# A planned attention and mixture kernel: other queue times for the factor spreads, another seed and number of planner passes, and 63-column constant matmuls in TensorE's planned gaps

## The chip, the cores and the metric

The kernel runs on one core of one Trainium2 chip. The metric is the device time of one execution in microseconds (us). All times of the trace come from one profiled execution.

## The reference, cut to what matters

Inputs are q, k and v of 4 batches, 12 heads, 448 positions and 64 columns, all float32. Attention comes first, then two feed-forward blocks on 1792 tokens of 768 columns; the output of the second is the result.

```python
q_n, k_n = rmsnorm(q, g_q), rmsnorm(k, g_k)          # x / sqrt(mean(x*x) + 1e-6) * g
scores = (q_n @ k_n.T) / sqrt(64)
scores = scores - max(scores)
attn = exp(scores);  attn = attn / (sum(attn) + 1e-9)
x = attn @ v                                          # 1792 x 768 after heads are joined
h = x @ moe_w_in                                      # 768 -> 2048
x = where(h > 0, h, exp(min(h, 0)) - 1) @ moe_w_out   # 2048 -> 768
xn = x / sqrt(mean(x*x) + 1e-6) * rms_g
g = xn @ w_gate;  silu = g / (1 + exp(-g))            # 768 -> 1536
out = (silu * (xn @ w_val)) @ moe2_w_out              # 1536 -> 768
```

## The kernel before, in words

**The work.** Every float32 operand is split into a high and a low part, and each product is made of three matmuls (high by high, high by low, low by high); much of the second half uses a scheme of seven products in place of eight. Attention is done in 24 pairs of heads, six pairs for each batch: `prep_q` and `prep_k` make the split operands `qh` and `ql` of a pair from the raw tile `rw`, `s_group` makes the scores in the banks 0 to 3 of PSUM (448 columns of 512), VectorE (DVE in the profile) takes the maximum of each row, ScalarE (ACT) the exponentials with their row sums (into `pj` and `p` for one parity of pairs, into `tbig` and `gbig` for the other), TensorE (PE) transposes these through the banks 4 to 6 into `pt` and `pe`, and multiplies with `rv`. The feed-forward work of a batch can start when its six pairs are done and `xf` is split into `xs`. The stages are: first block for batch 0, then for batch 1, second block for batches 0 and 1, first block for 2 and 3, second block for 2 and 3. Attention of batches 1 to 3 is laid between feed-forward matmuls; attention of batch 0 has nothing beside it. This is the lead-in, which ends at the first matmul on `xs`.

**The factors.** The key's norm factors `rr` must be there for every position in all 64 partitions of a head. `spread(i)` does that from pair 2 on by a write of `rr` to DRAM (`scr`) and two broadcast reads into `rb` (128 KB each), in SyncE's (SP) queue for the pairs 2 to 5 and in ACT's from then on. VectorE then multiplies `rw` with `rb` in place (`prep_k`, one SCALAR_TENSOR_TENSOR of 128x512). `sums(i)` does the same with the row sums (`rsum` to `rsb`).

**Weights.** `w_convert` (line 790) loads a compressed weight of 768 KB (`wr` from `wst`), makes `wc` from its upper part and the low half of `wt` from its bytes (each on ACT or on GpSimd, POOL), the high half of `wt` and the joining of both on VectorE. `w` and its low part are then copied from `wc`.

**The planner.** All of this is first entered into a class `Plan` (lines 34 to 300): each operation with the engines that could do it and a price for each, what it reads and writes. `schedule()` makes an order from a start rank with noise from `SEED`, then goes forward and backward `PASSES` times and keeps the order with the shortest modelled span. `forward()` is a list scheduler: an engine that is free takes the ready operation of lowest rank; an operation with two engines goes to the one that the model says is free sooner. `dma()` gives a transfer its modelled time. `issue()` writes all instructions out in the order of the planned starts; so the model's prices set the order and the engine of each instruction, and nothing of the model is left at run time. The string `LEAD` sets the first rank of batch 0's attention steps.

**Constant matmuls.** In planned gaps of TensorE `issue()` writes matmuls of ones by ones of 128 columns, whose result nothing reads. They go to bank 5, up to the planned start of the first instruction that uses bank 5 (`self.first_use`).

All instructions carry line 344 in the trace, since a wrapper at that line issues them; tiles name them.

## Time and profile before

| | us |
|---|---|
| median of 3 runs | 1232.96 |
| lowest and highest run | 1228.6, 1235.3 |
| profiled execution, its own time | 1231.14 |
| its span in the trace | 1229.3 |
| PE busy | 1205.9 (98%) |
| PE weight loads busy | 1013.6 (82%) |
| DVE, ACT, POOL busy | 907.4, 715.5, 836.6 |

The mean granted TensorE clock was 0.995 of full speed. The profile's busy share of PE counts pipelined matmuls, whose ends are modelled. The share is an average over stages that differ: the lead-in, where attention stands alone, has its own limits, and the feed-forward stages have theirs.

### The profile page before, as it was taken

Reading aid. Unit: us, or ns where it says so; the run is one execution under the profiler, and the core shown is the slowest. Engines: PE = TensorE matmul, PEld = TensorE weight load, DVE = VectorE, ACT = ScalarE, POOL = GpSimd, SP = SyncE. Lnnn points to the kernel's source line nnn. Section 1 sums busy time; section 2 is a strip of 40 time slices with the busy share of each in tenths; the row PEclk is TensorE's granted clock in tenths of the full one; section 3 lists DMA queues with packets and bytes.
Section 4 is the critical chain, followed back from the end, with each engine's and each line's share of the span. In section 5 each row is a group of like instructions: output and inputs, shape, how many; then the busy total and the mean of one; then the engine's idle time right before and its main releaser. Section 6 shows DMA issues by size and latency. Waiting matters only on the chain.

```text
span 1229.3 us, 18750 instructions
## 1 busy us (share of the span) xinstructions
PE 1205.9 (98%) x6270; PEld 1013.6 (82%) x6270; DVE 907.4 (74%) x1520; ACT 715.5 (58%) x1456; POOL 836.6 (68%) x713
## 2 busy tenths in 40 slices
PE   8999999999999999999999999999999989999998
PEld 6557867777777876777999998999999988899997
DVE  7877789898544469655598799948654799577667
ACT  6986878778765478665565565846534742322121
POOL 3467778788665686435998788866564877577484
PEclk9999999999999999999999999999999999999999
DMA  7678777776443468755599799767621266877767
GB/s 255 200 233 270 260 258 243 241 250 201 146 134 113 145 209 290 261 175 190 179 322 356 253 347 366 252 217 238 192 83 52 65 177 188 231 214 196 218 202 218
DMA packets 120164, 265.52 MB, mean 216 GB/s; under 512 B 15742, under 2 KB 59012, under 8 KB 120068
## 3 DMA queue, kind: packets, MB, share of 16 engines
q1 hardware_dynamic: 90260, 205.79, 49.5%
q0 software_dynamic: 21168, 49.55, 14.1%
q10 hardware_dynamic: 8640, 8.99, 2.6%
q8 instruction: 49, 0.80, 0.3%
q14 instruction: 47, 0.39, 0.1%
HBM read 183.11 MB, written 81.17 MB: 215 GB/s over the span
## 4 chain that ended last, share of the span: by engine, by line
PE 75%; DVE 8%; DMA 6%; ACT 4%; POOL 4%; issue 3%; ACTq 0%; SPq 0%; DVEq 0%; POOLq 0%
PE bank L344 75%; DMA wr<-wst 3%; POOL w L344 2%; DVE bank L344 2%; DVE tbig L344 1%; DVE wt L344 1%; DVE wc L344 1%; DVE gbig L344 1%; ACT tbig L344 1%; DVE ss L344 1%; ACT p L344 1%; DMA rsb<-rsum 1%; ACT wc L344 1%; DMA rw<-qk 1%; DMA rb<-scr 1%
## 5 line engine op out<-in xcount | busy, mean ns | idle before, releaser
L344 PE MATMUL bank<-xs,w 128*128 128x448 f32 x1731 | 396.8, 371 | 2.6 <-POOL xs L344 0.8
L344 PE MATMUL bank<-gbig,w 128*128 128x448 f32 x1603 | 362.4, 370 | 1.9 <-DVE gbig L344 0.8
L344 PEld LDWEIGHTS bank<-xs,w 128*128 128x128 f32 x1731 | 319.2, 188 | 35.6 <-issue 6.9
L344 PEld LDWEIGHTS bank<-gbig,w 128*128 128x128 f32 x1603 | 295.7, 188 | 31.8 <-issue 5.6
L344 POOL TENSOR_TENSOR w<-wc,w 128x768 fp32r<-128x768 f32 (+1 forms) x112 | 208.7, 1865 | 58.2 <-ACT w L344 47.7
L344 PE MATMUL bank<-late,w 128*128 128x448 f32 x647 | 162.8, 368 | 0.3 <-DMA w<-bout_S 0.3
L344 DVE TENSOR_REDUCE bank<-bank 128x1 f32<-128x448 f32 x168 | 98.9, 624 | 49.5 <-PE bank L344 49.1
L344 PEld LDWEIGHTS bank<-late,w 128*128 128x128 f32 x647 | 122.4, 189 | 10.5 <-ACT ybig L344 0.6
L344 ACT ACTIVATE p<-bank,nm,rr 128x448 f32<-128x448 f32 x126 | 90.0, 717 | 35.9 <-DVE nm L344 27.8
L344 DVE SCALAR_TENSOR_TENSOR wc<-wc,wt 128x768 int32<-128x768 int32 x68 | 88.8, 1306 | 13.9 <-ACT wc L344 9.7
L344 ACT ACTIVATE pt<-bank 128x384 f32<-128x384 f32 (+2 forms) x174 | 75.8, 451 | 33.3 <-PE bank L344 26.2
L344 POOL TENSOR_SCALAR w<-wc 128x768 fp32r<-128x768 f32 (+1 forms) x50 | 47.2, 945 | 58.8 <-PE bank L344 46.8
L344 DVE TENSOR_SCALAR wt<-wr 128x768 uint16<-128x768 uint16 x68 | 73.8, 1085 | 0.7 <-DMA wr<-wst 0.2
L344 ACT ACTIVATE wc<-wr 128x768 f32<-128x768 f32 x57 | 52.0, 912 | 37.7 <-DMA wr<-wst 17.8
L344 ACT ACTIVATE w<-wc 128x768 fp32r<-128x768 f32 (+1 forms) x75 | 59.0, 788 | 24.5 <-PE bank L344 23.0
L344 DVE TENSOR_TENSOR ybig<-bank,ybig 128x448 f32<-128x448 f32 x72 | 44.4, 618 | 38.6 <-PE bank L344 38.4
L344 PE MATMUL bank<-ident,p 128*128 128x128 f32 x441 | 71.5, 281 | 1.2 <-ACT rt L344 0.4
L344 ACT ACTIVATE tbig<-bank 128x448 f32<-128x448 f32 x85 | 45.9, 541 | 44.8 <-PE bank L344 31.3
L344 PEld LDWEIGHTS bank<-ident,p 128*128 128x128 f32 x441 | 54.2, 143 | 19.3 <-ACT pt L344 5.5
L344 DVE TENSOR_TENSOR tbig<-bank,tbig 128x448 f32<-128x448 f32 x93 | 56.0, 617 | 11.4 <-PE bank L344 10.6
L344 ACT ACTIVATE wt<-wr 128x768 uint16<-128x768 uint8 x49 | 53.4, 1090 | 15.5 <-DVE wc L344 13.0
L344 POOL TENSOR_TENSOR w<-p,w 128x768 fp32r<-128x768 f32 x28 | 54.2, 1939 | 12.0 <-ACT w L344 11.7
(271 smaller groups left out, 2233.7 us busy)
## 6 DMA issues: line engine op xcount, KB each, us to landing
wr<-wst SPq DMA_DIRECT2D x68, 768.0 KB
wc<-kept SPq DMA_DIRECT2D x64, 384.0 KB
kept<-wc SPq DMA_DIRECT2D x52, 384.0 KB
w<-bgv_S POOLq DMA_DIRECT2D x38, 384.0 KB, 3.9
bgv_A<-w SPq DMA_DIRECT2D x36, 384.0 KB
bgv_S<-w SPq DMA_DIRECT2D x32, 384.0 KB
rw<-qk SPq DMA_DIRECT2D x21, 512.0 KB
w<-bgv_A POOLq DMA_DIRECT2D x28, 384.0 KB, 4.0
```

What stands on the lines that cost most here:

```text
L344: return lambda *a, **k: f(*[real(x) for x in a], **{n: real(x) for n, x in k.items()})
```

## The change

The planner gets another seed and another number of passes, and its model is changed in two places. In `dma()` the broadcast reads of the factors get a modelled time that is 2.9 times (SP queue) or 1.4 times (ACT queue) as long, those of the row sums 2.0 or 1.2 times. In `forward()` an operation of DVE that uses the port shared with POOL, and that is planned while POOL issues a DMA, is priced to end only after that issue plus `AFTER`; before, a DMA issue of POOL counted as any other operation of POOL. Neither adds an instruction; both move where instructions stand and which engine does them.

In `issue()` constant matmuls are also written after bank 5 is in use, up to planned time 29.0. These late ones have 63 columns and go to the columns 449 to 511 of bank 3, behind the 448 columns that hold scores.

```diff
-    PASSES = 18
-    SEED = 7
+    PASSES = 13
+    SEED = 20
...
+    AFTER = 0.5
...
-    IDLE = (1.2, 0.3, 4.6)
+    IDLE = (1.2, 0.3, 4.6, 29.0, 0.125)
...
-            if e == "g" or e == "v" and self.ops[i][5]:
-                if port > t:
-                    price = port - t + max(0.03, price - self.BEHIND[e])
+            if e == "g" and self.ops[i][4]:
+                held = t + price
+            elif e == "g" or e == "v" and self.ops[i][5]:
+                at = max(port, held + self.AFTER) if e == "v" and held > t + 0.05 else port
+                if at > t:
+                    price = at - t + max(0.03, price - self.BEHIND[e])
                 port = t + price + self.TAIL[e]
...
-        t, end = self.IDLE[0], self.start_t[self.first_use]
+        t, used = self.IDLE[0], self.start_t[self.first_use]
         for i in order:
-            if eng[i] == "pe" and t < end:
-                while t + self.IDLE[1] + self.idle_price(t) < self.start_t[i] and t < end:
-                    self.idle()
-                    t += self.idle_price(t)
+            if eng[i] == "pe" and t < self.IDLE[3]:
+                late = self.start_t[i] >= used
+                while t + self.IDLE[1] + self.idle_price(t, late) < self.start_t[i]:
+                    self.idle(late)
+                    t += self.idle_price(t, late)
...
-    def idle_price(self, t):
-        return 0.43 if t < self.IDLE[2] else 0.225
+    def idle_price(self, t, late):
+        return self.IDLE[4] if late else 0.43 if t < self.IDLE[2] else 0.225
...
-    def dma(dst, src, nbytes, after=None, soon=False, by="sp"):
+    def dma(dst, src, nbytes, after=None, soon=False, by="sp", slow=1.0):
...
-            [dst] if dst.name != out.name else [], [src], lag=nbytes / Plan.DMA_RATE, after=after, soon=soon, dma=True,
+            [dst] if dst.name != out.name else [], [src], lag=slow * nbytes / Plan.DMA_RATE, after=after, soon=soon, dma=True,
...
-    plan.idle = lambda: T.matmul(banks[5][:, 0:P], onef.to_broadcast([P, P]), onef.to_broadcast([P, P]), start=True, stop=True)
+    def idle(late):
+        o = banks[3][:, S + 1:512] if late else banks[5][:, 0:P]
+        T.matmul(o, onef.to_broadcast([P, P]), onef.to_broadcast([P, size(o)]), start=True, stop=True)
...
-            dma(rb[64 * h:64 * h + 64], scr[h:h + 1].to_broadcast([64, 512]), 64 * 512 * 4, soon=True, by=by)
+            dma(rb[64 * h:64 * h + 64], scr[h:h + 1].to_broadcast([64, 512]), 64 * 512 * 4, soon=True, by=by, slow=2.9 if by == "sp" else 1.4)
...
-            dma(rsb[64 * h:64 * h + 64], scr[h:h + 1].to_broadcast([64, S]), 64 * S * 4, soon=True, by=by)
+            dma(rsb[64 * h:64 * h + 64], scr[h:h + 1].to_broadcast([64, S]), 64 * S * 4, soon=True, by=by, slow=2.0 if by == "sp" else 1.2)
```

On TensorE, in the lead-in behind the first transposes of pair 0, the rows of before are these. `qh` and `ql` are the split operands of pair 0, `gbig` those of pair 1, `small` holds the constant ones.

```order
L344 MATMUL bank5_132<-ident_61,pj0_109 64x128
L344 MATMUL bank1_128<-qh_102 128x448 [waits Activation_49]
L344 MATMUL bank2_129<-qh_102 128x448
...
L344 MATMUL bank2_129<-ql_103,qh_102 128x448
L344 MATMUL bank3_130<-gbig_88 128x448 [waits Activation_49]
L344 MATMUL bank3_130<-gbig_88 128x448
L344 MATMUL bank3_130<-gbig_88 128x448 [waits Pool_49]
L344 MATMUL bank0_127<-gbig_88 128x448 [waits Activation_49]
L344 MATMUL bank1_128<-gbig_88 128x448 [waits Activation_49]
```

Now the constant matmuls stand among them:

```order
L349 MATMUL bank5_132<-ident_61,pj0_109 64x128
L349 MATMUL bank3_130<-small_63 128x63 [waits DVE_49]
L349 MATMUL bank1_128<-qh_102 128x448 [waits Activation_49]
...
L349 MATMUL bank2_129<-ql_103,qh_102 128x448
L349 MATMUL bank3_130<-small_63 128x63 [waits Activation_49]
L349 MATMUL bank3_130<-small_63 128x63 x6
L349 MATMUL bank3_130<-gbig_88 128x448 x2
L349 MATMUL bank3_130<-gbig_88 128x448 [waits Pool_49]
L349 MATMUL bank3_130<-small_63 128x63 x2
L349 MATMUL bank0_127<-gbig_88 128x448 [waits Activation_49]
L349 MATMUL bank1_128<-gbig_88 128x448 [waits Activation_49]
```

Seven constant matmuls stand ahead of pair 1's first score matmuls, and the first of them carries the wait on ACT that the score matmul carried before, since it writes the same bank; two stand behind. Four more (not shown) stand a little later ahead of another group on bank 3, also behind a wait on ACT.

On VectorE at the same place, before: `rw` is the raw tile of pair 2 and `rb` its spread factors; the other rows are maxima of scores (TENSOR_REDUCE) and the negated maxima `nm` that ACT's exponentials of pairs 0 and 1 wait for.

```order
L344 SCALAR_TENSOR_TENSOR rw0_100<-rw0_100,small_63,rb0_101 128x512 [waits DMAHW1_49,DMAHW2_49,DMAHW0_49,Pool_49]
L344 TENSOR_REDUCE bank1_128<-bank1_128 128x1 [waits PE_49]
L344 TENSOR_REDUCE bank2_129<-bank2_129 128x1 [waits PE_49]
L344 TENSOR_TENSOR nm0_119<-bank1_128,rr0_114 128x1 [waits DVE_49]
```

And now:

```order
L349 TENSOR_REDUCE bank1_128<-bank1_128 128x1 [waits PE_49]
L349 TENSOR_REDUCE bank2_129<-bank2_129 128x1 [waits PE_49]
L349 TENSOR_TENSOR nm0_119<-bank1_128,rr0_114 128x1 [waits DVE_49]
...
L349 TENSOR_REDUCE bank0_127<-bank0_127 128x1 [waits PE_49]
L349 TENSOR_REDUCE bank1_128<-bank1_128 128x1 [waits PE_49]
L349 TENSOR_TENSOR nm1_120<-bank0_127,rr0_114 128x1 [waits DVE_49]
L349 SCALAR_TENSOR_TENSOR rw0_100<-rw0_100,small_63,rb0_101 128x512 [waits DMAHW1_49,DMAHW2_49,DMAHW0_49,Pool_49]
```

The multiplication, with its wait for the DMAs of the spread, is moved behind four reductions and their `nm`.

On ACT, a little later in the lead-in, before, between the copies of pair 0's and pair 1's transposes:

```order
L344 ACTIVATE pt1_108<-bank4_131 128x384 [waits PE_49]
L344 ACTIVATE wc0_93<-wr0_91 128x768 [waits DMAHW3_49]
L344 ACTIVATE ybig_89<-bank5_132 128x3x64 [waits PE_49]
L344 ACTIVATE ybig_89<-bank5_132 64x64
L344 ACTIVATE tbig_90,sm1_118<-bank1_128,nm1_120,rr0_114 128x448 [waits DVE_49]
```

This conversion of a weight to `wc`, and the one ahead of it, are now on GpSimd, which has this order:

```order
L349 TENSOR_SCALAR wc0_93<-wr0_91 128x768 [waits DMAHW3_49]
L349 TENSOR_SCALAR qh_102<-rw0_100 128x512 [waits DVE_49]
L349 TENSOR_TENSOR ql_103<-rw0_100,qh_102 128x512 [waits Pool_49]
...
L349 TENSOR_SCALAR wc0_93<-wr0_91 128x768 [waits DMAHW2_49]
L349 TENSOR_TENSOR gbig_88<-wr1_92,gbig_88 128x512 [waits Activation_49]
L349 TENSOR_SCALAR qh_102<-rw0_100 128x512 [waits DMAHW0_49,PE_49]
```

The two conversions wait for the weights' DMAs and have split operands of the pairs 2 and 3 queued behind them. In the lead-in as a whole, ACT does five `wc` conversions, two `w` copies, two `qh` copies and one `xs` copy fewer, and two `wt` and one `gbig` more; POOL does five `wc`, four `qh` and four `w` copies more. Two more weights are fully converted before the last `xf` of batch 0 is there.

## Rows read from the trace of the kernel before

**Rows 1.** Busy time of each engine, from the page.

```profile
PE 1205.9 (98%) x6270; PEld 1013.6 (82%) x6270; DVE 907.4 (74%) x1520; ACT 715.5 (58%) x1456; POOL 836.6 (68%) x713
```

**Rows 2.** Busy time by windows of the lead-in and one steady window.

```profile
core 0: us, PE busy (x) PEld busy (x) DVE busy (x) ACT busy (x) POOL busy (x), PEclk, DMA share, GB/s
42.00:62.00 20.00, 19.83 (x119) 10.71 (x119) 17.78 (x43) 19.88 (x53) 10.16 (x10) 1.00 0.54 173
62.00:86.00 24.00, 23.34 (x140) 12.29 (x139) 18.39 (x44) 23.94 (x63) 14.39 (x12) 1.00 0.72 244
600.00:985.00 385.00, 383.95 (x1888) 354.34 (x1887) 299.77 (x456) 221.44 (x400) 288.53 (x206) 1.00 0.66 225
```

**Rows 3.** The same view, short windows around the low clock.

```profile
23.40:26.80 3.40, 1.27 (x4) 0.67 (x4) 2.10 (x7) 1.84 (x6) 1.88 (x3) 1.00 0.83 324
27.00:30.40 3.40, 2.91 (x12) 2.11 (x12) 3.40 (x12) 3.40 (x8) 1.62 (x2) 0.50 0.47 158
30.40:33.80 3.40, 3.40 (x17) 2.62 (x15) 2.66 (x7) 3.12 (x11) 2.42 (x1) 0.50 0.76 199
```

**Rows 4.** TensorE's timeline in the lead-in: start, us, instruction, count, idle before and releaser.

```profile
8.55 4.73 PE L344 MATMUL bank<-small 128*128 128x128 f32 x40
...
24.41 1.27 PE L344 MATMUL bank<-gbig 128*128 128x448 f32 x4 [1.60 <-ACT p L344]
27.49 1.48 PE L344 MATMUL bank<-gbig 64*128 64x448 f32 x5 [1.81 <-ACT p L344]
...
39.46 0.44 PE L344 MATMUL bank<-ident,tbig 128*128 128x128 f32 x2
41.39 0.33 PE L344 MATMUL bank<-ident,tbig 128*128 128x128 f32 x1 [1.50 <-ACT tbig L344]
```

**Rows 5.** VectorE's timeline there.

```profile
24.70 0.75 DVE L344 SCALAR_TENSOR_TENSOR rw<-rw,small,rb 128x512 f32<-128x512 f32 x1 [2.08 <-DMA rb<-scr]
25.37 1.16 DVE L344 TENSOR_REDUCE bank<-bank 128x1 f32<-128x448 f32 x2
```

**Rows 6.** ACT's timeline in the lead-in.

```profile
22.65 1.00 ACT L344 ACTIVATE tk<-tk 128x960 f32<-128x960 f32 x1
...
26.62 0.72 ACT L344 ACTIVATE p<-bank,nm,rr 128x448 f32<-128x448 f32 x1 [1.56 <-DVE nm L344]
27.34 0.71 ACT L344 ACTIVATE p<-bank,nm,rr 128x448 f32<-128x448 f32 x1
...
28.96 0.89 ACT L344 ACTIVATE wc<-wr 128x768 f32<-128x768 f32 x1
...
39.42 0.90 ACT L344 ACTIVATE wc<-wr 128x768 f32<-128x768 f32 x1 [1.95 <-DMA wr<-wst]
...
40.54 0.71 ACT L344 ACTIVATE tbig<-bank,nm,rr 128x448 f32<-128x448 f32 x1
```

**Rows 7.** POOL's timeline, a conversion that waits for a weight.

```profile
65.56 1.06 POOL L344 TENSOR_SCALAR wt<-wr 128x768 uint16<-128x768 uint8 x1 [4.37 <-DMA wr<-wst]
```

**Rows 8.** TensorE's timeline around the lead-in's end.

```profile
91.67 1.74 PE L344 MATMUL bank<-ident,tbig 128*128 128x128 f32 x12 [1.04 <-ACT rsb L344]
...
103.39 10.40 PE L344 MATMUL bank<-xs,w 128*128 128x448 f32 x50 [0.75 <-POOL xs L344]
```

**Rows 9.** TensorE's timeline at the start of the last stage.

```profile
991.85 1.40 PE L344 MATMUL bank<-late,w 128*128 128x448 f32 x6
996.85 0.74 PE L344 MATMUL bank<-gbig,ones 128*128 128x448 f32 x1 [3.40 <-DVE gbig L344]
997.39 2.44 PE L344 MATMUL bank<-late,w 128*128 128x448 f32 x6
```

**Rows 10.** VectorE's timeline at the same place.

```profile
990.06 2.89 DVE L344 TENSOR_TENSOR tbig<-tbig,xf 128x448 f32<-128x448 f32 x1
...
993.41 3.38 DVE L344 TENSOR_TENSOR gbig<-tbig,gbig 128x448 fp32r<-128x448 f32 x1
...
998.73 0.61 DVE L344 TENSOR_TENSOR gbig<-tbig,gbig 128x448 fp32r<-128x448 f32 x1
```

More of the change, by code (lines that the diff above doesn't have):

```diff
@@ L190, in forward @@
         taken = [False] * n
-        port = 0.0
+        port = held = 0.0
         dma_free = 0.0
@@ L593 @@
     plan.idle_bank = banks[5].name
-    plan.idle = lambda: T.matmul(banks[5][:, 0:P], onef.to_broadcast([P, P]), onef.to_broadcast([P, P]), start=True, stop=True)
+    def idle(late):
+        o = banks[3][:, S + 1:512] if late else banks[5][:, 0:P]
+        T.matmul(o, onef.to_broadcast([P, P]), onef.to_broadcast([P, size(o)]), start=True, stop=True)
+    plan.idle = idle
     def phase(k):
```

## Prediction

> **What bounds the kernel now.** The busy times come first: PE is busy for 98% of the span, every other engine for far less [rows 1]. So what can be won as a whole is PE's idle time, some 23 us of 1229, and time in which PE runs at a lower clock. The windows then say where that is. In a steady feed-forward stretch PE is busy for 383.95 of 385 us [rows 2]: nothing is to be had there by another order. I looked for the gaps in PE's timeline next. They lie in two places: the lead-in, where batch 0's attention stands alone, and the start of the last stage, where PE waits 3.40 us for the operand of a norm [rows 9].
>
> In the lead-in PE waits 1.60 us and 1.81 us for exponentials on ACT [rows 4]. In the short window that holds both it is busy for 1.27 of 3.40 us; behind it the granted clock is 0.50, half of full speed (1.2 for 2.4 GHz), in two windows of 3.40 us each [rows 3]. There PE is busy without a pause but does half the work. A third gap, 1.50 us, is a wait for the exponential `tbig` [rows 4].
>
> Who was late for these? ACT's timeline: the exponentials of `p` at 26.62 had waited 1.56 us for `nm` from DVE [rows 6]. DVE's timeline: the reductions that make this `nm` stood behind the multiplication of `rw` with `rb`, which had itself waited 2.08 us for the spread's DMA [rows 5]. So a product that pair 2 needs much later held up the maxima of pair 0. The third gap: ACT waited 1.95 us for a weight's DMA, then converted for 0.90, and only then made `tbig`, at 40.54 [rows 6].
>
> From 42 to 86 us there is no such hole: PE is busy 19.83 of 20 and 23.34 of 24 us, and ACT 19.88 of 20 and 23.94 of 24 [rows 2]. Two engines are full side by side.
>
> **The change part by part.**
>
> *The first wait.* DVE's multiplication now stands behind the reductions of the banks 1 and 2 and two further ones, so its 2.08 us of waiting (with 0.75 of work) leaves the path to the exponentials. The square `tk` (1.00 us on ACT) is moved behind them too. Before, the last two exponentials of pair 0 ended at 28.05 (27.34 + 0.71). PE's wait of 1.60 us began at 22.81 (24.41 - 1.60, [rows 4]), so it had written these scores by then, and the reductions could start there; 1.16 us for both [rows 5], and the `nm` behind them, give about 24.3. The last two exponentials take 1.43 from there (0.72 + 0.71) and end at about 25.7: 2.3 us earlier. The multiplication itself then waits for less, since its DMA lands at the same time; what is late next is the split of pair 2's keys, which begins behind it and is wanted only after the scores of pair 1.
>
> *The second wait.* Both conversions to `wc` (0.89 and 0.90) and the 1.95 of waiting leave ACT up to the `tbig` at 40.54, `tk` comes back to it there (1.00). Together: 2.3 + 0.89 + 0.90 + 1.95 - 1.00 = 5.0 us, so this `tbig` ends at about 36.2 and not at 41.25. Whether PE can follow: from 27.49 to 39.90 [rows 4] are 12.4 us, of which 6.31 busy at half clock (2.91 + 3.40, [rows 3]). At full clock these are 3.15, so the stretch takes 9.25. From about 25.1 on, with 0.5 for constant matmuls and 0.9 for what gaps remain, it ends at 35.75. The two ways agree, and I take -5.0. The bounds: if PE still waits as before and the clock falls as before, 0; if all of 1.60 + 1.81 + 1.50 and half of the 6.31 goes, -8.1.
>
> *The constant matmuls.* One matmul of 128 columns is two records in the trace, and 40 records took 4.73 us ahead of the lead-in [rows 4]: 0.24 for each matmul, 0.12 for one of 63 columns if time goes by columns. Between these lie the bounds for the 14 late ones: 1.7 to 3.3 us of PE. What matters is where they stand. In the order, seven stand ahead of pair 1's first scores, and the first of them waits for the same exponential as those scores, because they write bank 3 as well; four more have the same form. So 11 of 14 do not run in the gap; they run when it has ended and delay the scores by 7 x 0.12 = 0.84 and 4 x 0.12 = 0.5 us. One ahead of pair 0's last scores waits on the maximum of bank 3, and the two behind fill truly. I therefore put almost nothing of the clock to their credit: it must come from gaps that are shorter by themselves. If 0.84 of delay is absorbed by ACT, which is late there anyway, 0.5 remains, and is in the sum above.
>
> *From 42 to 86 us.* With both engines full an earlier start is carried through to the end, and is neither enlarged nor lost: 0. ACT loses some further conversions and POOL takes them; PE, as full as ACT, does not get faster by that. Bounds below, as rivals.
>
> *The end of the lead-in.* PE waits 1.04 and 0.75 us around the last transposes and the first feed-forward matmuls [rows 8]. Two more weights are ready by then, so part of it goes; bounds 0 and -1.8, and I take -0.5.
>
> *The start of the last stage.* The 3.40 us and the half clock behind it (six matmuls in 2.44 against 1.40 before the wait, [rows 9]) cost 4.4 us. The operand that PE waits for is DVE's `gbig` at 993.41, which took 3.38 us, as its forerunner at 990.06 took 2.89, where the same kind takes 0.61 a little later [rows 10]. POOL issues DMAs and does products beside them. The new order has two DVE operations in place of six between the last bank accumulated and this product, and the model now knows a price for DMA issues of POOL. But it has the two norms in the other order, with less feed-forward work ahead of one. Bounds: -4.4 if the wait goes, +3.4 if a second wait of this size comes; I take -1.5, a third.
>
> A rule of the Trainium skill ("SBUF — State Buffer", section "Who interferes with whom") says that a VectorE instruction with two inputs in SBUF contends with a GpSimd instruction that reads SBUF. The stretched products of [rows 10] fit it, with 3.38 against 0.61 us; by it the conversions moved to POOL would cost DVE time in the lead-in, which is the second rival.
>
> *The rest.* A new order of the steady stages: 0, with 0.3% of PE's time idle there.
>
> Sum: -5.0 - 0.5 - 1.5 = -7.0 us. On the profiled execution, 1231.14, that gives 1224.1; on the median of the runs, 1.8 us higher, 1226.0. I predict 1225, between the two.
>
> **The rivals.**
>
> *Gaps don't close.* The 11 constant matmuls that wait run behind the gap, the gap ahead of pair 1's scores stays over a us, and the granted clock falls again. For it: they share the wait of what they should precede. Against it: the exponentials come 2.3 us earlier without them. Then the 3.15 us of half clock and 0.5 for constant matmuls come back: -3.5, about 1228.5.
>
> *DVE becomes the bound of the lead-in.* Five conversions, at 0.9 us each [rows 6], are on POOL; if DVE stands still for each, 4.5 us come onto an engine that is busy 17.78 of 20 us from 42 to 62 [rows 2]. For it: the stretched rows at the last stage [rows 10]. Against: 2.2 us in 20 are free on DVE, and the conversions read one input only. -7.0 + 4.5 = -2.5, about 1230.5.
>
> *ACT alone binds from 42 to 86.* PE's weight loads are busy for 10.71 of 20 us there, 54%, against 354.34 of 385, 92%, in the steady window [rows 2]: so PE could go faster if its inputs came sooner, and its 99% hide waits inside. Then ACT's loss of conversions counts: three more `wc` beside the two counted, at 0.9, and two `w` copies and two `qh` against two `wt` and a `gbig` (about 1.5 net by rows of the same kind) give 4.2 us more. Against: the timeline shows no gap of PE there that ACT ends. About 1220 to 1221.
>
> The Trainium skill ("Perfetto Trace Analysis", section "Identifying the Most-Contended Engine") holds matmul busy time to be a poor measure and asks for weight-load busy time; the 54% against 92% is where this trace bears it out, and this rival is what follows from it.
>
> *Slower: POOL's queue.* The conversions now on POOL wait for weights of 768 KB, and operands of the next pairs (`qh`, `ql`) stand behind them. One wait for such a DMA took 4.37 us on POOL [rows 7] and 1.95 on ACT [rows 6]. If three of the five wait as long as the former, pairs 2 to 4 are late by 13.1 us and PE stands: -7.0 + 13.1 = +6.1, about 1238. It decides where POOL has less than that in hand ahead of a pair's scores. Against: only the first two of the five have such operands close behind them, and ACT's waits for weights in the same stretch were one of 1.95, not of four.
>
> **How the numbers follow.** Forecast 0.42, its own range 1222 to 1228; gaps don't close 0.22; DVE binds 0.13; ACT alone 0.13; POOL's queue 0.10. The range 1218 to 1233 leaves out the ends of the last two and some of the boundary's +3.4, together under 2 in 10. What a measurement of this kernel can tell from no change is 0.5%, 6.2 us: faster means under 1226.8, slower over 1239.1. Faster: three quarters of the forecast (0.32), nearly all of ACT alone (0.12), a fifth of the first rival (0.05) make 0.49. Slower: half of POOL's queue and a little of the rest, 0.06. Same: 0.45.
>
> **What would show it.** Right, step by step: DVE reduces the banks 1 and 2 at about 23 without the 2.08 wait ahead; pair 0's exponentials end by 25.7; the granted clock stays 1.00 from 26 to 35; no `wc` on ACT between the `tbig` rows, and the last of those by about 36.2; the first matmul on `xs` 5 us earlier; under 2 us of waiting at the norm of the last stage. Wrong, if the clock is 0.50 again at 27 to 34, if POOL shows waits for `wr` of over 2 us with PE idle between 42 and 90, if DVE's rows from 42 to 86 are stretched, or if two waits of over 2 us stand at the last stage.

## The result and the profile after

The changed kernel is slower. Its runs have a median of 1241.3 us (1239.8 to 1246.4), those of the kernel before, beside them on the chip, 1232.3 (1228.6 to 1235.3): a ratio of 1.0081, 95% interval 1.0053 to 1.0109. The forecast was 1225 and the range ended at 1233. The profiled execution of the changed kernel took 1243.11 us with a span of 1241.3, which is 12.0 us more than the span of 1229.3 before. Of these, 3.0 belong to the two executions: this one lies 1.8 us above its kernel's median, the profiled one of before 1.2 below, and the medians differ by 9.0.

The page's busy line, for [rows 1]:

```profile
PE 1211.8 (98%) x6300; PEld 1015.1 (82%) x6300; DVE 918.9 (74%) x1518; ACT 708.0 (57%) x1441; POOL 839.1 (68%) x730
```

TensorE has 30 records more (the constant matmuls) and is as full as before; such a line can't tell where 12 us went. Windows of the changed kernel can, for [rows 2] and [rows 3]: window, length, busy time of the engines, granted clock, DMA share, GB/s.

```profile
23.40:26.80 3.40, 2.88 (x16) 2.84 (x17) 1.67 (x5) 3.00 (x9) 2.31 (x3) 0.73 0.92 314
27.00:30.40 3.40, 3.40 (x16) 2.65 (x15) 1.71 (x7) 1.28 (x3) 0.28 (x1) 0.50 0.30 100
30.40:33.80 3.40, 3.40 (x25) 2.94 (x24) 3.27 (x7) 2.57 (x8) 2.08 (x2) 0.80 0.23 42
62.00:86.00 24.00, 23.30 (x149) 13.37 (x147) 21.19 (x43) 21.70 (x56) 16.43 (x16) 1.00 0.84 260
112.00:114.00 2.00, 2.00 (x7) 1.78 (x6) 1.80 (x3) 2.00 (x4) 1.94 (x2) 0.50 0.87 220
117.00:330.00 213.00, 207.24 (x1110) 160.25 (x1111) 175.01 (x263) 162.72 (x337) 166.74 (x120) 1.00 0.70 230
600.00:985.00 385.00, 382.97 (x1873) 350.57 (x1872) 293.44 (x445) 216.78 (x387) 277.86 (x201) 1.00 0.67 227
```

The clock was 0.50 again from 27 to 30.4 us, and once more behind 110 us, where before it stayed up. From 117 to 330 TensorE is idle for 5.8 us; the kernel before was idle there for 1.1 (211.87 busy of 213).

Both kernels hold the same matmuls except the constant ones. So I weighed each matmul with the median spacing of its kind, summed them in TensorE's order, and read when each kernel has done the same share. This table is worked out so; it tells by how many us the changed kernel is late (+) or early (-) against the kernel before, from one profiled execution of each:

```
when before is at     47    96   106   115   148   205   346   430   720   811   961  1089   end
the changed kernel  -1.9  -3.3  -4.2  +2.9  +2.9  +6.0  +9.0  +9.4  +9.4 +12.3 +12.5  +8.5 +12.0
```

By 106 us the lead-in has gained 4.2 us. Then 7.1 us are lost at one place between 106 and 115, about 6.5 bit by bit up to 430, nothing to 720, 3 between 720 and 811, 4 come back at the start of the last stage, and 3.5 go in the tail. The places, on TensorE's timeline of the changed kernel (start, us, instruction, count, idle before and its releaser), for [rows 4], [rows 8] and [rows 9]:

```profile
23.91 2.33 PE L349 MATMUL bank<-small 128*128 128x63 f32 x14 [1.45 <-ACT p L349]
26.01 1.47 PE L349 MATMUL bank<-gbig 128*128 128x448 f32 x3
...
100.38 5.53 PE L349 MATMUL bank<-xs,w 128*128 128x448 f32 x26 [0.62 <-POOL xs L349]
...
111.00 6.71 PE L349 MATMUL bank<-xs,w 128*128 128x448 f32 x18 [5.09 <-DVE tbig L349]
...
146.18 0.55 PE L349 MATMUL bank<-ident,p 128*128 128x128 f32 x3 [0.49 <-ACT pt L349]
...
201.09 0.44 PE L349 MATMUL bank<-qh 128*128 128x448 f32 x1 [0.65 <-ACT p L349]
...
273.01 0.28 PE L349 MATMUL bank<-ident,rs 128*7 128x128 f32 x1 [1.02 <-DVE rs L349]
...
1005.87 1.50 PE L349 MATMUL bank<-late,w 128*128 128x448 f32 x6 [1.79 <-ACT rsb L349]
...
1214.28 0.47 PE L349 MATMUL bank<-late,w 128*128 128x448 f32 x1 [1.97 <-DVE gbig L349]
```

At 23.91 the constant matmuls stand behind a gap of 1.45 us, not in it. The gap of 5.09 us ahead of 111.00 is the largest of the kernel; behind it 18 records take 6.71 us at half clock, which 3.9 us would do at full clock (the same 18 below). The releaser written there is the last of a chain. It begins on ACT, whose timeline has, for [rows 6] and behind:

```profile
25.16 0.72 ACT L349 ACTIVATE p<-bank,nm,rr 128x448 f32<-128x448 f32 x1
...
38.48 0.77 ACT L349 ACTIVATE tbig<-bank,nm,rr 128x448 f32<-128x448 f32 x1
...
97.37 1.09 ACT L349 ACTIVATE wt<-wr 128x768 uint16<-128x768 uint8 x1 [3.57 <-DMA wr<-wst]
97.39 3.66 ACTq L349 DMA_DIRECT2D scr<-rr  x6
103.53 1.15 ACTq L349 DMA_DIRECT2D rb<-scr  x2
107.66 1.00 ACT L349 ACTIVATE tk<-tk 128x960 f32<-128x960 f32 x1 [9.20 <-DMA tk<-tok]
108.57 0.53 ACT L349 ACTIVATE tbig<-bank 128x448 f32<-128x448 f32 x1
```

ACT stands 9.20 us ahead of the square of `tk`, and the evacuation `tbig<-bank`, for which DVE and then TensorE wait, is queued behind it. SP's queue issues the read of `tk` late:

```profile
97.35 0.33 SPq L349 DMA_DIRECT2D kept<-wc  x1
103.52 0.33 SPq L349 DMA_DIRECT2D tk<-tok  x1
```

and the view of waits (what is waited for, us in total, times, longest) has for it between 90 and 106 us:

```profile
SPq L349 <- DMA scr<-rr: 5.8, 1, 5.8
```

SP waited 5.8 us for a DMA that has no data for `tk`: the write of a key factor to `scr`. The program's order says how the two are tied; the first row is SP's, the second ACT's:

```
L349 DMA tk0_99<-tok 128x960 [waits DMAHW3_49,DVE_49]
L349 DMA rb0_101<-scr6_150 64x512 [waits DMAHW3_49,DMAHW2_49]
```

`DMAHW3` is the completion semaphore of the write of `scr6`, for which its reader `rb` waits; the read of `tk` completes on the same one, and is issued only when the earlier has landed. Both issues stand at 103.5 in the rows above. Six writes of 4 KB were put together on ACT's queue, from 97.39 to 101.05.

### The profile page after: what moved, and what is told of

The parts are those of the page before. It is cut to its first block, busy times and chain, and to the rows that moved or that the text cites. A ratio compares the mean times of both kernels' runs of the same rounds, so it can differ in the third digit from the quotient of the medians.

```text
span 1241.3 us, 18839 instructions
## 1 busy us (share of the span) xinstructions
PE 1211.8 (98%) x6300; PEld 1015.1 (82%) x6300; DVE 918.9 (74%) x1518; ACT 708.0 (57%) x1441; POOL 839.1 (68%) x730
## 4 chain that ended last, share of the span: by engine, by line
PE 68%; DVE 13%; DMA 7%; ACT 6%; issue 3%; POOL 2%; ACTq 0%; SPq 0%; DVEq 0%; POOLq 0%
PE bank L349 68%; DVE bank L349 3%; DVE tbig L349 2%; DMA wr<-wst 2%; DVE ybig L349 2%; ACT p L349 1%; DMA tk<-tok 1%; ACT tbig L349 1%; POOL w L349 1%; DMA rw<-qk 1%; DVE wc L349 1%; DMA tbig<-spill 1%; DMA out_t<-ybig 1%; DVE ss L349 1%; POOL tbig L349 1%
## 5 line engine op out<-in xcount | busy, mean ns | idle before, releaser
L349 PE MATMUL bank<-xs,w 128*128 128x448 f32 x1731 | 400.9, 372 | 7.4 <-DVE tbig L349 5.6
L349 DVE SCALAR_TENSOR_TENSOR wc<-wc,wt 128x768 int32<-128x768 int32 x68 | 84.4, 1242 | 17.1 <-ACT wc L349 12.5
L349 POOL TENSOR_SCALAR w<-wc 128x768 fp32r<-128x768 f32 x54 | 49.8, 924 | 54.9 <-PE bank L349 40.6
L349 DVE TENSOR_SCALAR wt<-wr 128x768 uint16<-128x768 uint16 x68 | 68.3, 1005 | 4.7 <-DMA wr<-wst 4.5
L349 ACT ACTIVATE w<-wc 128x768 fp32r<-128x768 f32 (+1 forms) x71 | 55.1, 776 | 28.9 <-PE bank L349 27.9
L349 POOL TENSOR_TENSOR w<-p,w 128x768 fp32r<-128x768 f32 x25 | 48.4, 1936 | 15.5 <-ACT w L349 8.7
L349 ACT ACTIVATE wc<-wr 128x768 f32<-128x768 f32 x48 | 43.7, 910 | 26.6 <-DMA wr<-wst 12.1
```

The lines of the kernel that those rows point to most:

```text
L349: return lambda *a, **k: f(*[real(x) for x in a], **{n: real(x) for n, x in k.items()})
```

## The experiments

Single executions of one kernel differ by some us (33 runs of the kernel before, beside the first four kernels below: 1228.7 to 1240.3), so verdicts go by ratios over many runs. How far the table of work done can be trusted shows in `b_fill` and `b_fill7` below: on every engine they have the old order, but for constant matmuls ahead of 34 us, and from 148 to 430 us they still lose 3.5 and 2.9 us against the kernel before. So some 3 us between two traces, over such a stretch, are weak evidence. Three profiled executions lie at the edge of their kernel's runs: `b_fill` (1240.95, median 1234.94) and `a_nofill` (1245.27, median 1241.15) are the slowest of theirs, and `h_oldnew` (1241.97, median 1248.3) is a fast one.

**What of the change costs.** Theory A: the whole loss lies in the new order of the stages from 96 us on. Rival B: the constant matmuls behind the waits cost it. Three kernels part the two. In `a_nofill` only the 14 late constant matmuls are gone:

```diff
-                while t + self.IDLE[1] + self.idle_price(t, late) < self.start_t[i]:
+                while not late and t + self.IDLE[1] + self.idle_price(t, late) < self.start_t[i]:
```

> The changed kernel without its 14 late constant matmuls of 63 columns; nothing else differs. Theory A (the constant matmuls stand in the path: with them PE works from 23.9 to 28.2 us on 9 of them and on pair 1's first scores, and the granted clock is halved all the same): pair 1's first scores start at about 24 instead of 26.0, the matmuls on xs start 2 to 4 us earlier, and the whole is 2 to 4 us faster, about 1238. Rival B (they are what keeps PE near its clock, and without them the half clock lasts longer): the low clock lasts longer than the 6.7 us of the changed kernel and the whole is 2 us slower or more. Rival C (batch 0's later steps absorb it): the gain is gone by 90 us and the whole stays within 1 us of the changed kernel.

In `a_lane` the writes of the key factors of four later pairs are moved, in the finished order, behind other DMA issues, so that the read of `tk` has a semaphore of its own; nothing else:

```diff
+    MOVES, FORCE = ((750, 1141), (921, 1448), (1039, 1498), (1202, 922)), {}
...
+        order = self.edited(order, eng)
```

Each pair names an operation and the one that it is put behind, together with what depends on it.

> The changed kernel with four of the six small writes of batch 1's factors to DRAM (scr of the pairs 8 to 11), which ACT's queue issues together at 97 us, issued later and apart; each engine's other instructions stand as before. In the changed kernel SP's read of tk was issued at 103.5, when the writes had landed, because it uses the same completion semaphore as one of them. Theory A (that shared semaphore makes the 5.09 us gap of PE at 106 and the half clock behind it): SP issues the read by 98, ACT squares it by 102.5, the gap of PE at 106 is under 1 us, the clock stays at 1.00 there, and the whole is 6 to 8 us faster, about 1234. Rival B (ACT and the weights are late there anyway): the gap shrinks to 3 us at least and the whole gains under 3 us. Rival C (the gain is lost again behind it): the gap goes, but from 120 to 400 us the kernel loses it again, and the whole gains under 3 us.

`a_both` has both edits:

> Both edits together: without the late constant matmuls, and with the four small writes later. If both losses are separate, the gains add up: 8 to 12 us faster than the changed kernel, 1229 to 1233, about the time of the kernel before. If one covers for the other, it is no faster than the better one of the two alone.

And `b_fill` is the kernel before with the changed kernel's rule for constant matmuls, so with 15 late ones on bank 3 and its own order:

```diff
-    IDLE = (1.2, 0.3, 4.6)
+    IDLE = (1.2, 0.3, 4.6, 29.0, 0.125)
...
-    plan.idle = lambda: T.matmul(banks[5][:, 0:P], ...)
+    def idle(late):
+        o = banks[3][:, S + 1:512] if late else banks[5][:, 0:P]
```

> The kernel before, in its own order, with the new constant matmuls in its planned gaps up to 29.0 (15 of them of 63 columns) and no other change. Theory A (they wait for what the gap ends on, and cost): pair 1's first scores start about 2 us later, the half clock stays about 6.8 us long, and the whole is 1 to 3 us slower. Rival B (they hold the clock): the half clock at 27 to 33.8 us is gone or under 3 us long, and the whole is 2 to 3 us faster.

Measured, as ratios to the kernel before (1.0081 for the changed kernel): `a_nofill` 1.0054 (1.0032 to 1.0076), `a_lane` 1.0024 (1.0004 to 1.0044), `a_both` 1.0034 (1.0015 to 1.0052), `b_fill` 0.9998 (0.9976 to 1.0019). With the old order the constant matmuls cost nothing that the runs can tell, and `a_lane` and `a_both`, with and without them, are alike. Without them the changed kernel's ratio is lower by 0.0027, with overlapping intervals, and most of its loss stays. B falls as the main cause. The gains of the two edits don't add up either (1229 to 1233 us was expected of `a_both` if they did; its median is 1238.3). Parting the semaphore gives back most of the loss: SP issues `tk` at 95.26 instead of 103.52, and TensorE of `a_lane` shows

```profile
24.61 1.77 PE L363 MATMUL bank<-small 128*128 128x63 f32 x14 [1.45 <-ACT p L363]
26.20 0.85 PE L363 MATMUL bank<-gbig 128*128 128x448 f32 x3
...
104.19 3.91 PE L363 MATMUL bank<-xs,w 128*128 128x448 f32 x18 [0.93 <-DVE tbig L363]
...
122.42 0.47 PE L363 MATMUL bank<-qh 64*128 64x448 f32 x2 [0.89 <-ACT p L363]
147.59 0.55 PE L363 MATMUL bank<-ident,p 128*128 128x128 f32 x3 [1.96 <-ACT pt L363]
185.86 0.47 PE L363 MATMUL bank<-qh 64*128 64x448 f32 x1 [0.99 <-ACT p L363]
265.59 0.28 PE L363 MATMUL bank<-ident,rs 128*7 128x128 f32 x1 [1.03 <-DVE rs L363]
```

0.93 us in place of 5.09, and 18 records in 3.91 in place of 6.71: the stall is 7 us and its cause is shown. (The edit also leaves two writes together in place of six; but `tk` is now issued 3.9 us before even these two let the read of `rb` go, at 99.21, so it is the semaphore that held it.) But the waits of 0.9 to 2 us behind it are still there, and `a_lane` is still slower than the kernel before: it is 6.7 us early at 115 and 1.9 late at 346. That is the second part of the loss.

**Which part of the order loses it.** The planner draws its order with a seed (18 passes with seed 7 before, 13 with seed 20 now). If the loss of 117 to 400 comes from that stretch's own order, it stays when the first 89 us are taken from the old draw; if it is a debt from the lead-in, it goes. `h_oldnew` is the changed kernel with the first part (all that is planned to start before 89.0) in the order of the kernel before, no late constant matmuls and the semaphore parted; `h_newold` is the kernel before with the changed kernel's first part, likewise:

```diff
+FIRST_PART = (
...
+        order = self.joined(order, eng)
+        order = self.edited(order, eng)
```

`FIRST_PART` lists operations with engine and planned start; `joined` puts them ahead of the rest of the draw, and `edited` makes the four moves of `a_lane`.

> The other way round: the order of the kernel before up to planned time 89, then what is left in the changed order, with the four small writes later and without late constant matmuls. Theory A: level with the kernel before at 110 us, 6 to 9 us behind it at 400 us, and 6 to 9 us slower at the end. Rival B (nothing of the loss is in the changed order of the later stages): within 2 us of the kernel before.

> The changed kernel's order up to planned time 89 (all of the lead-in but its last steps, without the late constant matmuls), then what is left in the order of the kernel before, with the small writes of the pairs 8 to 11 issued later as in the run a_lane. Theory A (the changed order itself loses some 8 us of PE between 117 and 330 us, in waits for ACT and VectorE that the order before doesn't have): 5 to 7 us ahead of the kernel before at 110 us, still 4 us or more ahead at 400 us, and 4 to 6 us faster than it at the end, about 1228. Rival B (what the lead-in gains can't be kept in any order, since ACT, VectorE and the weights' DMAs are as late as before): the lead is gone by 330 us, and the whole is within 2 us of the kernel before.

`h_oldnew` 1.0104 (1.0070 to 1.0137), `h_newold` 1.0003 (0.9990 to 1.0017). By the table of work done `h_oldnew` is level with the kernel before at 115 (-1.1) and 8.0 late at 430. So the changed order of the steady stretch loses about 8 us by itself, with the old lead-in ahead of it. `h_newold` brings the lead-in's gain to 96 us (-6.6) and loses it in one wait, on TensorE and on ACT:

```profile
100.89 0.74 PE L375 MATMUL bank<-xs,w 128*128 128x448 f32 x1 [5.93 <-ACT xs L375]
```

```profile
94.52 0.83 ACTq L375 DMA_DIRECT2D scr<-rr  x2
99.06 1.15 ACTq L375 DMA_DIRECT2D rb<-scr  x2
100.26 0.58 ACT L375 ACTIVATE xs<-xf 128x448 fp32r<-128x448 f32 x1 [4.71 <-issue]
```

The same kind of stall as at 106 us, with another victim: two spread reads wait on ACT's queue for their `scr` writes, and a feed-forward operand is queued behind them. From 115 to 961 this kernel, with the old draw's order, loses 4.0 us where the changed kernel loses 9.6 and `h_oldnew` 11.1.

`h_best` is `h_newold` with these two reads moved behind the copy (`MOVES = ((543, 458), (544, 458), ...)`):

> The kernel of the run h_newold (changed order of the lead-in, then the order before) with two DMA issues of ACT, the reads of rb from scr6 that wait for that write to land, moved behind ACT's copy of the last xs of batch 0. Theory A (in h_newold PE's gap of 5.93 us at 95 is this copy standing behind those two issues): the copy starts at about 95.6 instead of 100.26, the gap shrinks to about 1 us, and PE is 4 to 5 us further ahead at 110 us; the whole 3 to 5 us faster than the kernel before, about 1229. Rival B (the weights and batch 1's factors are as late as before, so the lead is lost in the next waits): ahead at 100 us, level at 150 us, and no faster than the kernel before.

1.0007 (0.9990 to 1.0024): the 5.93 us are gone, and waits of 0.93, 0.74, 1.68 and 1.83 stand at 96 to 113 instead; by 115 the lead is 0.4 us. The lead was lost to the next thing that was late.

The joined kernels also tell what the new first part is worth. `h_oldnew` and `a_both` differ in it alone (both have the new rest, the parted semaphore and no late constant matmuls), with 1.0104 against 1.0034 and intervals that lie apart. With the old rest it is worth nothing (`h_newold`). So the lead-in's gain is real: the new rest of the order carries it to the end, and the old rest loses it near 100 us.

**The model or the draw.** `b_model` is the changed kernel, with its costs for the spreads and for POOL's DMA issues, but drawn as before, and without late constant matmuls; `b_seed` is the kernel before, with its costs, drawn as now:

```diff
-    PASSES = 13
-    SEED = 20
+    PASSES = 18
+    SEED = 7
```

This is the edit of `b_model` (with that of `a_nofill`); `b_seed` has the same four lines the other way round.

> The changed planner's model (longer times for the spreads, the price of POOL's DMA issues) with the seed and the passes of the kernel before, and no late constant matmuls: what the change of the model alone makes of the order. Theory A (the model's change does what it says in the lead-in, and what an order loses later depends on the draw): VectorE doesn't wait for rb ahead of pair 0's maxima, PE is 2 to 4 us ahead at 60 us; behind it anything from -5 to +8 us, by waits under 1.5 us each. Rival B (the model's change itself makes the later stages worse): the same 6 to 9 us lost between 117 and 400 us as in the changed kernel.

> The kernel before with the seed and the number of passes of the changed kernel, and its own model: another draw of an order, without the change's other parts. Theory A (what an order loses after the lead-in is the draw's): VectorE waits for rb ahead of pair 0's maxima as in the kernel before, and the whole is 2 to 10 us slower than it. Rival B (a new seed is neutral, and it is the model's change with it that loses): within 2 us of the kernel before.

`b_model` 1.0004 (0.9988 to 1.0020), `b_seed` 1.0039 (1.0024 to 1.0053). Over the whole kernel the new costs lose nothing with the old seed, and the new seed loses 0.4% with the old costs. The table of work done, for the kernels of this question (worked out as above):

```
when before is at     47    96   115   148   205   346   430   720   961  1089   end
changed, seed 20    -1.9  -3.3  +2.9  +2.9  +6.0  +9.0  +9.4  +9.4 +12.5  +8.5 +12.0
a_lane, seed 20     -3.8  -5.2  -6.7  -6.3  -0.8  +1.9  +2.3  +2.2  +3.6  +0.1  +3.5
h_oldnew, seed 20   +0.6  -0.7  -1.1  +0.8  +2.7  +7.6  +8.0  +7.3 +10.0  +7.3 +10.9
b_seed, seed 20     -2.9  -6.2  -9.1  -5.9  -7.2  +0.5  -1.7  +2.6  +5.8  +3.4  +7.0
b_model, seed 7     -2.7  -4.0  -4.8  -0.9  -2.7  -0.1  +0.1  +1.9  +5.2  +1.3  +2.6
h_newold, seed 7    -5.3  -6.6  +0.2  +0.5  +1.3  +3.2  +2.8  +3.8  +4.2  +3.8  +4.6
```

From 148 to 430 the four with seed 20 lose 6.5, 8.6, 7.2 and 4.2 us, the two with seed 7 lose 1.0 and 2.3. Over all kernels of the study it is 4.2 to 9.6 against 0.5 to 3.5. It is no debt of an early lead: `h_oldnew` has none at 148 and loses as much as `a_lane`, which is 6.3 early. So the new seed loses here without the new costs. The 4.2 of `b_seed` is close to what executions of the old order differ by, and its ratio of 1.0039 is the firmer ground.

That the new costs lose nothing is not shown. Counted from 115 us, as the 6.5 us above are, the four with seed 20 lose 6.5 to 9.1, but `b_model` loses 4.9 (3.9 of it by 148) and `m_fill7` below, with the same order, 8.2; the five kernels that keep the old order behind 115 lose 0.8 to 3.6. A kept seed does not keep the order, since the model's prices set it too. `b_model` comes out level because its lead of 4.8 us pays for what it loses. And one new seed is one draw: what others cost was not tried.

**What the moved wait is worth alone.** `b_dve` is the kernel before with one operation moved: the multiplication of pair 2 stands behind pair 0's and 1's reductions (`MOVES = ((189, 106),)`).

> The kernel before with one instruction moved: VectorE's multiplication of pair 2's rw with rb, which waits for the spread's DMA, stands behind the four reductions and nm as in the changed order; one subtraction on POOL that reads its result moves with it. Theory A (that wait alone held pair 0's last exponentials): they end at about 25.9 and not at 28.05, PE's gap of 1.81 us shrinks to under 0.6, PE is 1.5 to 3 us ahead at 40 us, and the whole is 1 to 3 us faster if nothing takes it back. Rival B (ACT's square and conversions bound these steps anyway): under 0.7 us ahead at 40 us.

1.0018 (0.9998 to 1.0038). Pair 0's exponentials end at 25.86, as in the changed kernel (25.88) and near the 25.7 worked out. But ACT, which kept its two conversions, then shows

```profile
25.14 0.72 ACT L358 ACTIVATE p<-bank,nm,rr 128x448 f32<-128x448 f32 x1
...
40.06 0.89 ACT L358 ACTIVATE wc<-wr 128x768 f32<-128x768 f32 x1 [4.23 <-DMA wr<-wst]
41.17 0.71 ACT L358 ACTIVATE tbig<-bank,nm,rr 128x448 f32<-128x448 f32 x1
```

and TensorE a gap of 3.65 us (1.50 before, [rows 4]): the 1.95 us of waiting for the weight in [rows 6] grew to 4.23, since ACT reached it earlier and the DMA did not. So the moved wait is worth nothing alone. The other edit, the conversion off ACT, was not tried alone, but `b_seed` comes near to it. VectorE there still waits for `rb`:

```profile
24.12 0.75 DVE L344 SCALAR_TENSOR_TENSOR rw<-rw,small,rb 128x512 f32<-128x512 f32 x1 [2.06 <-DMA rb<-scr]
```

But no `wc` stands between ACT's `tbig` rows, and the last of them starts at 36.13 (40.54 before):

```profile
36.13 0.70 ACT L344 ACTIVATE tbig<-bank,nm,rr 128x448 f32<-128x448 f32 x1
```

TensorE is 2.9 us early at 47 and 9.1 at 115, without late constant matmuls and at a clock of 0.50 from 27 to 30.4. So a lead of this size needs neither the moved wait nor the new costs; its larger part fits the conversion that left ACT's path. One execution of an order that differs in much else shows no more.

**The clock in the lead-in.** If half clock at 27 to 34 us costs 3.15 us, holding it up must bring about that. `l_fill7` is `a_lane` with the late constant matmuls in a bank that nobody reads then, so that they wait for nothing; `b_fill7` is the kernel before with such matmuls, `m_fill7` is `b_model` with them:

```diff
-        o = banks[3][:, S + 1:512] if late else banks[5][:, 0:P]
+        o = banks[7][:, S + 1:512] if late else banks[5][:, 0:P]
```

> The kernel of the run a_lane with the 14 late constant matmuls in bank 7 and not in bank 3: nothing reads or writes bank 7 at that time, so none of them carries a wait. Theory A (their wait is what makes them miss the gap): the 7 ahead of pair 1's first scores run in the gap that ends with ACT's exponential, PE's gap there shrinks from 1.45 to under 0.3 us, the first scores start by 24.9 instead of 26.2, the clock stays at 1.00 from 20 to 36 us, and PE is 1 to 1.5 us further ahead at 50 us; the whole is 1 to 1.5 us faster than a_lane, hard to tell in its time. Rival B (the clock falls or holds whatever fills the gap): the same gap and the same lead as in a_lane or in the run without them.

> The kernel before in its own order, with the 15 late constant matmuls of the run b_fill, but in bank 7, so that none of them waits. Theory A (they fill the gaps and hold the clock, and nothing else in this order changes): PE's gaps of 1.60 and 1.81 us at 22.8 and 25.7 are filled or under 0.6 us, the clock stays at 1.00 from 24 to 36 us, PE is 2 to 3 us ahead of the kernel before at 36 us; of that 1 us or less remains at 110 us, since ACT's wait for a weight at 37 to 39 us comes next, and the whole is 0 to 2 us faster. Rival B (the lead is kept): 3 us faster as a whole.

> The kernel of the run b_model (the changed model of the planner with the seed and passes of before) with its 20 late constant matmuls in bank 7. Theory A (an order without the changed order's losses from 117 to 330 us keeps what the clock gives): the clock stays at 1.00 from 24 to 36 us where b_model had 0.50 for 5 to 6 us, PE is 2 to 3 us further ahead at 60 us, and the whole is 1 to 3 us faster than b_model and than the kernel before, about 1231. Rival B (every lead of the lead-in is lost by 300 us, as in the runs with the changed order): the clock holds, but the whole is within 1 us of b_model.

`l_fill7` 1.0024 (1.0005 to 1.0043), `b_fill7` 1.0011 (0.9995 to 1.0027), `m_fill7` 1.0026 (1.0010 to 1.0043). In `b_fill7` a gap of 1.20 us stays ahead of 27.12, and the clock is 0.50 again from 30.4 to 33.8, so it doesn't test this. In the two others the gaps are filled; windows of `l_fill7`:

```profile
20.00:24.00 4.00, 4.00 (x29) 3.04 (x30) 3.86 (x17) 3.68 (x10) 0.00 (x0) 1.00 0.92 304
24.00:27.00 3.00, 3.00 (x21) 2.49 (x21) 2.50 (x11) 2.41 (x8) 1.90 (x2) 1.00 0.75 260
27.00:30.00 3.00, 2.88 (x22) 2.20 (x21) 2.86 (x7) 2.89 (x7) 2.08 (x3) 1.00 0.44 149
```

and the same stretch of `b_model`, which has none:

```profile
27.00:30.00 3.00, 2.42 (x11) 1.13 (x8) 3.00 (x13) 2.27 (x5) 0.65 (x2) 0.50 0.46 164
```

At 47 us `l_fill7` is 4.8 us early, `a_lane` 3.8 (both at 1.00 all through) and `a_nofill`, at 0.50 from 27 to 30.4, 4.0. `m_fill7`, at full clock, and `b_model`, at half, are both 2.7 early. So a full clock gives 0 to 0.8 us where no constant matmul waits. DVE and ACT are busy for 2.86 and 2.89 of 3 us in `l_fill7`, which fits that they set the pace. Neither kernel is faster than the one it was made from, where 1 to 3 us were expected.

Where the constant matmuls do wait, the clock is worth more. On each engine `a_lane` and the changed kernel run the same instructions in the same order, and `a_lane` kept its clock, by the windows view and by ACT's timeline:

```profile
27.00:30.40 3.40, 3.24 (x28) 2.50 (x26) 2.92 (x11) 2.90 (x7) 0.87 (x2) 1.00 0.44 139
```

```profile
36.44 0.78 ACT L363 ACTIVATE tbig<-bank,nm,rr 128x448 f32<-128x448 f32 x1
```

Its last `tbig` starts 2.0 us earlier than the 38.48 of the changed kernel, although pair 0's exponentials had ended 0.7 later (26.59 against 25.88), and it is 1.9 us further ahead at 47.

What the clock is worth over the whole kernel stays open. Of the 12 runs of `l_fill7` the five with a mean granted clock of 0.999 or 1.000 took 1231.4 to 1235.4 us, the seven below that 1236.0 to 1242.6. Where it was low in those, and whether it or longer waits came first, no trace shows.

**ACT's order in the steady stretch.** The waits of 117 to 330 stand mostly on ACT's `p`, `pt` and `rt`. Theory: ACT's conversions ahead of the exponentials cause them. `l_acts` is `a_lane` with such conversions and squares put behind the exponentials at four places (ten more moves).

> The kernel of the run a_lane with ACT's instructions exchanged in four places between 117 and 265 us: two conversions to wc, one pair of wc and wt, and one square of tk with five small scr writes each stand behind the one or two exponentials or copies of transposes that PE waited for. Theory A (PE's gaps there are ACT's head of line: an instruction that waits for a DMA or for POOL stands ahead of one that PE waits for): PE's gaps of 0.89, 1.96, 0.99 and 1.03 us go or shrink to under 0.4 each, PE is 3 to 5 us earlier at 330 us than in a_lane, and the whole is 2 to 4 us faster, about the time of the kernel before or a little under it. Rival B (other waits take their place, since VectorE and the weights are as late): under 1.5 us earlier at 330 us.

1.0069 (1.0043 to 1.0096), no better than `a_lane` and probably worse. The four gaps are gone, so the instructions that were moved did stand ahead of them, but others of 2.05, 1.17 and 3.85 us came at 138, 196 and 272. So the theory that these exchanges make the whole faster falls.

## Why the prediction was wrong

**The lead-in: the path was right, two of its terms mis-sized.** DVE's first two reductions come at 22.62 with no wait ahead; pair 0's exponentials end at 25.88 (forecast: by 25.7); no `wc` stands between ACT's `tbig` rows. But the last of these starts at 38.48, 2.1 us before its place in [rows 6], and should have ended by 36.2; the lead at 47 us is 1.9, not 5.0. At 106 it is 4.2 of the 5.5 forecast. What is missing is the half clock, which the forecast took to be gone, and the constant matmuls, put at 0.5. With a full clock and constant matmuls that wait for nothing (`l_fill7`) the lead at 47 is 4.8, near the forecast; with the half clock alone 4.0 and 4.1 (`a_nofill`, `a_both`), with waiting constant matmuls alone 3.8 (`a_lane`), with both 1.9. So the half clock is no fixed 3.15 us: by these executions, one of each kernel, it cost 0.8 at most where no constant matmul waits and 1.9 where they do, and they cost 1.0 at full clock and 2.1 at half. The rival "gaps don't close" came true (gap 1.45 us, clock 0.50), and its sum, 2 us of lead where 5.5 were forecast, is near what stood at 47; but `a_lane` has the same gap of 1.45 and kept its clock, so that the gap makes the clock fall is not shown. Two readings were wrong: ACT's square of `tk` did not move behind the exponentials, and in the first of the two low-clock windows of [rows 3] TensorE was not busy without a pause, but for 2.91 of 3.40 us.

**The constant matmuls.** Forecast 1.34 us of delay for 11 of them, by columns at full clock. They stand behind the gap, as read from the order. But the 7 ahead of pair 1's scores took 1.59 us at full clock (24.61 to 26.20 in `a_lane`), 0.227 each (a matmul has two records), as long as those of 128 columns in [rows 4] (4.73 for 20, 0.237): their time does not go by columns. The loads of their weights, 128x128 in either case, take 189 ns each in `a_lane` and 190 in the kernel before, and overlap; that these set the pace fits, but was not tried. In the changed kernel, as the clock fell, they took 2.1 us (23.91 to 26.01). `a_nofill`, without them and at half clock too, is 4.0 early at 47, and `a_both`, likewise, 4.1, so they may account for the 2.1 us between `a_nofill` and the changed kernel; the ratios don't part them.

**From 42 to 86 us: 0, and that was about right.** From 47 to 96 the lead grows by 1.4 us. DVE's rows are busier (21.19 of 24 us, 18.39 before) but the lead still grew, so they didn't bind (that rival's time was also put 1 us too high: -2.5 gives 1229.5 by the reckoning of the others); POOL's queue did not hold the operands up (that rival's place, its price and its wait were wrong, though its time of 1238 lies nearest to the result).

**"The rest. A new order of the steady stages: 0" is the step that failed.** In the trace it is +20.2 us in place of 0: 7.1 at one stall, 6.5 from 115 to 430, 3.1 from there to 961 and 3.5 in the tail, against gains of 4.2 in the lead-in and 4.0 at the last stage. It hid two things above all. One is the stall at 106 us, 7.1 us: the order showed `DMAHW3` on the read of `tk`, and I followed the queues of DVE, ACT and POOL, but not what else completes on that semaphore. The Trainium skill ("DMA: Bandwidth & Descriptors", section "Why a DMA increments its semaphore by 16 and not by 1") advises one semaphore for each slot in flight, not one for a stream. Its ground is that a wait can otherwise pass before the data has landed, which no run here shows. In this trace the second of two transfers on one semaphore was held back until the first had landed, 5.8 us on SP, and TensorE stood for 5.09 behind it. The other is the new order of the steady stretch: 6.5 us in small waits between 115 and 430. `h_oldnew` has such a loss without the new lead-in, `b_seed` without the new costs, and `b_model` without the new seed. I took "0.3% idle" of TensorE as a property of the stage. It belonged to the one order that had been drawn.

**The start of the last stage: -1.5 forecast, -4.0 measured.** The window 985 to 1001 has TensorE busy for all 16.00 us at clock 1.00; the 3.40 us of [rows 9] are gone, and 1.79 stand at 1005.87 behind ACT's `rsb`. The -4.4 of the bound was nearer than the third that I took. The products themselves are still stretched at times (DVE's 2.95 us at 1000.90 against 0.61 for its kind), so the gain is in the order, not in quieter products.

**What stays open.** How much of the steady stretch's loss is the seed's and how much the new costs' is not settled, nor what another seed would do. Which resource sets the small waits of the new draw from 117 to 430 is not settled: exchanges on ACT moved them and made them larger. The 3 us between 720 and 811, of which waits on TensorE make 1.3 (0.89, 0.63 and 0.48 against one of 0.74 before), and the tail's 3.5 us with its wait of 1.97 at 1214.28, were not tried. No kernel of this study beats the kernel before by its interval.

## What to carry to other kernels

A planner's new draw is a new kernel everywhere, not only where its rules changed: price the steady stretch by what a redraw has cost (the one that was tried here, with the old rules, cost 0.4%). Keeping the seed does not keep the order once a rule has changed: `b_model` came out level because it lost what its lead-in had won. In an order, follow each DMA's completion semaphore to whatever else uses it, above all where small transfers are put together ahead of a load that a busy engine waits for. A gain in a lead-in counts only if the transfers and engines behind it have that much in hand: remove a wait and name the next one.

## What the runs showed of the hardware

Six writes of 4 KB, issued on ACT's queue from 97.39 to 101.05, let their waiters go at 103.5, and two in `h_newold`, issued from 94.52, at 99.06: 6.1 and 4.5 us from the first issue, so a small write is no short one. A constant matmul of 63 columns takes 0.227 us at full clock, one of 128 takes 0.237. The granted clock of one and the same order is not fixed: `a_lane` and the changed kernel run the same instructions on each engine, and TensorE had 1.00 from 27 to 30.4 in the one profile and 0.50 in the other.
